# A new order for the 2,617 steps of a fused attention and two-layer feed-forward kernel

## The chip, the cores and the metric

The kernel runs on one core of one Trainium2 chip, as one program. The metric is the time of the whole program on the device, in microseconds (us).

The engines of the core are called by these names: TensorE (PE in the rows, PEld for its weight loads) does the matmuls and the transposes, VectorE (DVE), ScalarE (ACT) and GpSimd (POOL) the elementwise work, and SyncE (SP) issues the DMAs. Each engine takes its own instructions strictly in the order of the program and waits on semaphores for the others.

## The reference, cut to what matters

```python
# q, k, v: 4 batches, 8 heads, 576 positions, 64 values; m = 32 landmarks
q_lm, k_lm = (x.reshape(B, H, m, S // m, D).mean(axis=3) for x in (q, k))
A  = softmax(scale * q    @ k_lm.T)      # 576 x 32
Bm = softmax(scale * q_lm @ k_lm.T)      # 32 x 32
C  = softmax(scale * q_lm @ k.T)         # 32 x 576
Z  = Bm.T / (norm1(Bm) * norminf(Bm) + 1e-06)
for _ in range(6):
    Z = 2 * Z - Z @ Bm @ Z
attn = A @ Z @ C @ v                     # -> x: 2304 tokens x 512

h = x @ w_in                             # first layer, 512 -> 2048
y = (h * tanh(log1p(exp(h)))) @ w_out    # 2048 -> 512
h = y @ w_in2                            # second layer
out = square(maximum(h, 0)) @ w_out2
```

## The kernel before, in words

The whole kernel is one list of short steps, the string PROGRAM at the top of the file. The last loop of the kernel takes the steps from left to right and calls the method that each names: `t11.e1` is method `e(1)` of object `t11`. A step issues from one to some tens of instructions, mostly on one engine. So the order of the list is the order of the instructions on every engine, TensorE's, VectorE's, ScalarE's and GpSimd's queues and SyncE's DMA queue alike; nothing else orders the work. What follows an `@` names the kind of PSUM buffer that a TensorE step takes, and `+n` puts n matmuls without use ahead of it.

Buffers are handed out while the list is run: a step that needs one takes the one that has been free for longest (`take`, line 253), and the step that reads last gives it back (`give`). There are 25 pages of 128x768 numbers (39 later), 24 buffers for weights, and five of PSUM: two of kind h, two of kind y, one of kind at. A step that takes a buffer waits on the chip until the readers of its former contents are done.

The objects are these.

- **a to h**: the eight groups of four heads. Loads (lk, lq, lv), sums for the landmarks (sk, sq), transposes on TensorE (tk, tq, tl, pe), scores and products (pa, pb, pc, pv), softmax and scaling on VectorE, ScalarE and GpSimd (cm, ce, at, am, mi, ae, su, mu, tb, ah, al).
- **B0, B1, B2**: the small inverse for batch 0, for batch 1, and for batches 2 and 3. nr, rs and bs prepare it; n0 to n5 are the Newton steps on TensorE, each with an r on ScalarE (line 747) and a z on VectorE (line 751); pw and wz finish it.
- **F00 to F33**: folds of the attention into the first layer's weights, for a batch and a quarter of the hidden units: fo on TensorE (line 797), mh on ScalarE, ml on VectorE (line 808).
- **U0 to U63**: weights of both layers. d loads one (SyncE); lo and ab (ScalarE, lines 329 and 338), st (VectorE, line 332) and cl (VectorE, lines 342 and 343) mend its bits, ad adds the halves on GpSimd; hi and lw split it into a high and a low part.
- **t0 to t23**: the first layer, by quarter of the hidden units and by tile of 384 tokens. f0 to f3 are matmuls into an h buffer, M the activation, c and g (line 885) the split in two parts, y0 to y3 the second matmuls, each into a y buffer, and e0 to e3 (line 926 on VectorE for most) add a y buffer to the sum and free it. With two y buffers, y3 waits for e1, and y0 of the next turn for e2.
- **W, K, X**: sums and differences of the second layer's weights (W0 to W7, K0 to K7) and of its input (X0 to X2). Their l steps are long subtractions on GpSimd (lines 953 and 992), the t steps of X differences on VectorE (line 983).
- **Q, Y, Z**: the second layer in three passes over the tokens. Qpj loads weights (a, b), does seven products P on TensorE (p1 to p7, lines 1191 to 1193) and adds them on VectorE (d1 to d7). Ypm loads weights (b), prepares its input (r, t on line 1064, h on ScalarE, l on GpSimd on line 1087), does seven products O (p1 to p7) and adds them (a1 to a7). Zp ends a pass and stores. Each O product is 18 matmuls and each P product 6.
- **x**: e and m load ScalarE's tables for Exp and Mish ahead of their use; two frees the buffers of the first half.

Every product is made of three matmuls of high and low parts (`prod`, lines 811 to 814).

Of the kernel before, what the change touches and what calls it, by code (L numbers as in the profile page):

```python
# [10 lines left out]
F32 = mybir.dt.float32  # L11
F32R = mybir.dt.float32r
U32 = mybir.dt.uint32
# [41 lines left out]
    B0.n2@at+2 U3.ab U2.cl f.lk B0.r2 c.Sk c.tl@y B0.z2 U3.cl c.TL d.tk@h a.tb U3.ad a.cv U7.ab b.pv@y+1 d.sk d.lv
    b.ae U2.ad a.ah c.pb@at B0.n3@y+2 c.PB d.Tk c.pc@h U7.cl c.lv B0.r3 d.Sk B0.z3 b.cr U7.ad B0.n4@y c.cm b.cv
    e.tk@h B0.r4 a.al B0.z4 c.ce b.su B0.n5@y d.tl@y d.TL c.pa@at e.lv B0.z5 U7.hi B0.pw@y+3 e.Tk c.at U7.lw d.pb@y
    c.am U5.lo d.pc@at b.mu U4.hi B0.wz d.cm F00.fo@h U4.lw b.tb d.ce e.sq b.ah d.pe@at b.al U8.d F00.mh f.tk@h+4
    f.lv d.PB d.ET d.pa@at F00.ml B1.bx B1.be d.pv@y U6.lo U5.st t0.f0 B1.bs U6.st c.mi B1.nr@y f.Tk e.Sq c.ae B1.rs
# [5 lines left out]
    h.lv U9.lo U11.st d.mu f.at d.tb F10.mh f.pc@h e.pa@at f.cm f.pb@y c.al d.ah U11.ab F10.ml t0.y3 f.ce U11.cl
    e.at e.pe@h t0.e3 f.PB d.al t1.f0 U9.st e.ET t1.f1 t1.f2 U9.ab g.lk t1.M0 e.cr t1.f3 f.pe@h t1.c0 t1.M1 U9.cl
    f.ET g.lq g.tk@at U11.ad t1.c1 U10.d f.am e.am U9.ad f.cr t1.g0 U10.lo t1.g1 U13.d U10.st g.Tk t2.f0 t2.f1
    U13.lo U10.ab e.mi e.pv@y U13.st e.cv f.pv@y g.tq@at U13.ab U10.cl U10.ad e.ae t1.y0 U13.cl f.cv U12.d t2.f2
    g.sk f.mi t2.f3 t1.e0 U13.ad t1.y1 g.sq t2.M0 F01.fo@h U13.hi g.Tq e.su g.Sk U12.lo g.Sq t1.e1 F01.mh U13.lw
# [20 lines left out]
    K1.v3 U23.ab t9.f1 K1.h1 t7.y0 t7.y1 K1.l0 t8.M1 U23.cl U40.lo U23.ad U40.st t7.e0 t7.e1 U23.hi K1.sv0 t9.f2  # L90
    U40.ab t7.y2 U23.lw t7.y3 U41.d U40.cl t7.e2 t8.c1 t7.e3 t8.g0 t8.g1 F31.ml U40.ad U22.d t9.f3 U41.lo t9.M0
    U41.st t8.y0 U41.ab U41.cl K1.l1 t8.y1 t9.M1 U41.ad t10.f0 K1.sv1 t8.e0 U22.lo U22.st U24.d U22.ab W2.v0 t8.e1
    t9.c0 t8.y2 U22.cl t8.y3 U22.ad t9.c1 t9.g0 U22.hi t8.e2 U24.lo t8.e3 t10.f1 t10.f2 U22.lw W2.v1 U24.st t10.f3
    W2.v2 U24.ab t9.g1 t10.M0 U31.d U31.lo U24.cl U31.st t11.f0 t9.y0 W2.v3 t10.M1 t11.f1 U24.ad U31.ab U31.cl x.m
    W2.h1 U26.d U31.ad t9.e0 t9.y1 U31.hi U26.lo t9.e1 t10.c0 W2.l1 t9.y2 U31.lw t9.e2 t10.c1 W2.sv1 U26.st t10.g0
    t11.f2 U16.d U26.ab t9.y3 U26.cl t11.f3 W2.h0 U26.ad t10.g1 W2.l0 t11.M0 t9.e3 U44.d t10.y0 W2.sv0 U16.lo U16.st
    t11.c0 U16.ab t10.e0 U16.cl U16.ad U45.d t10.y1 t10.y2 F02.fo@at t10.e1 t11.M1 U44.lo U44.st U44.ab t10.e2
    U44.cl t10.y3 F02.mh U45.lo F02.ml t11.g0 U44.ad t12.f0 U45.st t11.c1 U27.d t12.f1 U45.ab F12.fo@at F12.mh
    t11.g1 t10.e3 K2.v0 t11.y0 U45.cl F12.ml U27.lo U45.ad U27.st U27.ab K2.v2 t12.f2 t11.y1 t11.e0 t12.M0 U27.cl
# [5 lines left out]
    U46.st t12.y3 W3.l0 t12.e2 U46.ab W3.sv0 t14.M0 U47.lo U46.cl t13.y0 F32.mh t15.f0 t14.c0 U46.ad U47.st t12.e3
    U47.ab U28.d t14.M1 t15.f1 W3.h1 t13.e0 W3.l1 U47.cl U28.lo Q00.a0 t13.y1 t15.f2 t13.y2 t14.g0 t14.c1 F32.ml
    t13.e1 U47.ad U28.st K3.v0 t13.e2 F03.fo@at W3.sv1 t13.y3 K3.v1 U28.ab U28.cl Q03.a0 U28.ad U28.hi U28.lw K3.v3
    t15.M0 t15.f3 t13.e3 t14.g1 t14.y0 t14.e0 t15.c0 K3.v2 t15.M1 U48.d U48.lo t14.y1 U48.st K3.h1 t16.f0 t16.f1
    U49.d t14.e1 U48.ab t15.c1 U49.lo U48.cl U49.st K3.l1 t15.g0 t15.g1 t14.y2 K3.sv1 U48.ad t14.y3 U29.d U49.ab
# [1215 lines left out]
```

## Time and profile before

| | before |
|---|---|
| median of 3 runs | 796.95 us (791.98 to 797.18) |
| the profiled execution | 794.81 us |
| its span, first to last instruction | 793.0 us |
| TensorE busy | 763.4 us, 96% |
| VectorE busy | 613.5 us, 77% |
| ScalarE busy | 408.0 us, 51% |
| GpSimd busy | 439.0 us, 55% |
| mean granted TensorE clock | 0.997 |

The profiled execution is one run of the program. Its span leaves out 1.8 us around the first and the last instruction. TensorE's busy time is that of overlapping matmuls whose ends are modelled, so a busy TensorE is not always one at its full rate; a row of the profile gives the idle time of an engine just before an instruction and what ended it.

### The profile page before, as it was taken

The page shows a single profiled execution, that of the slowest core. Times are in us where ns is not written, and L with a number is a line of the kernel's source. Part 1 is how long each engine was busy: PE and PEld are TensorE (multiplying, and loading weights), DVE is VectorE, ACT ScalarE, POOL GpSimd, SP SyncE. Part 2 cuts the span into 40 slices and gives each one's busy share as a digit, 9 for nine tenths or more (in the row PEclk, how much of TensorE's full clock was granted, in tenths as well). Part 3 has the DMA queues.
Part 4 walks back from the last instruction along what each step waited for, and adds up shares of the span by engine and source line. Part 5 has one row for each costly group of instructions (what it writes and reads, how often), then busy time and mean ns, then how long its engine had stood idle before and what let it go on. Part 6 is the DMA issues. An engine that isn't in the chain of part 4 may idle for free.

```text
span 793.0 us, 15868 instructions
## 1 busy us (share of the span) xinstructions
PE 763.4 (96%) x6094; PEld 720.3 (91%) x6094; DVE 613.5 (77%) x920; ACT 408.0 (51%) x630; POOL 439.0 (55%) x287
## 2 busy tenths in 40 slices
...
GB/s 288 294 196 68 166 136 106 122 147 217 164 178 173 170 214 173 228 178 264 277 297 200 350 258 253 213 263 262 225 276 326 247 239 242 231 269 309 272 78 80
DMA packets 95596, 171.45 MB, mean 216 GB/s; under 512 B 10016, under 2 KB 37664, under 8 KB 95520
## 3 DMA queue, kind: packets, MB, share of 16 engines
...
q10 hardware_dynamic: 576, 0.79, 0.4%
...
q14 instruction: 28, 0.23, 0.1%
...
## 4 chain that ended last, share of the span: by engine, by line
PE 68%; DMA 10%; DVE 8%; ACT 7%; POOL 3%; issue 3%; SPq 0%; DVEq 0%; ACTq 0%; POOLq 0%
PE O L813 8%; PE O L814 8%; PE O L812 8%; PE P L1191 7%; PE P L1192 7%; PE P L1193 7%; DMA rawwi<-in_moe_w_in_dram 6%; PE y L812 5%; PE y L813 4%; PE y L814 4%; DMA rawwo<-in_moe_w_out_dram 3%; PE h L812 2%; PE h L814 2%; PE h L813 2%; DVE rawwi L332 1%
## 5 line engine op out<-in xcount | busy, mean ns | idle before, releaser
L1087 POOL TENSOR_TENSOR glr<-A,ghr 128x768 fp32r<-128x768 f32 x77 | 157.4, 2067 | 125.4 <-ACT ghr L1082 105.0
L812 PE MATMUL O<-b,ghr 128*128 128x256 f32 x462 | 130.3, 282 | 0.7 <-ACT ghr L1082 0.7
L813 PE MATMUL O<-b,ghr 128*128 128x256 f32 x462 | 130.5, 282 | 0.0
L814 PE MATMUL O<-b,glr 128*128 128x256 f32 x462 | 130.5, 282 | 0.0
L1082 ACT CAST ghr<-A 128x768 fp32r<-128x768 f32 x77 | 62.3, 835 | 117.8 <-DVE A L1064 48.8
L812 PEld LDWEIGHTS O<-b,ghr 128*128 128x128 f32 x462 | 87.9, 190 | 1.0 <-ACT ghr L1082 1.0
L813 PEld LDWEIGHTS O<-b,ghr 128*128 128x128 f32 x462 | 88.0, 190 | 0.3 <-DMA b<-sc 0.3
L814 PEld LDWEIGHTS O<-b,glr 128*128 128x128 f32 x462 | 88.2, 191 | 0.0
L812 PE MATMUL h<-ah,mh 128*128 128x384 f32 (+1 forms) x256 | 79.0, 309 | 0.0
L814 PE MATMUL h<-ah,ml 128*128 128x384 f32 (+1 forms) x256 | 78.0, 305 | 0.0
L813 PE MATMUL h<-al,mh 128*128 128x384 f32 (+1 forms) x256 | 78.0, 305 | 0.0
L1221 DVE TENSOR_TENSOR A<-U,P 128x384 f32<-128x384 f32 x88 | 47.9, 549 | 30.8 <-PE P L1193 29.2
L1221 DVE TENSOR_TENSOR U<-U,P 128x384 f32<-128x384 f32 x72 | 39.6, 551 | 39.7 <-PE P L1193 39.1
L885 DVE TENSOR_TENSOR gl<-s,gh 128x768 fp32r<-128x768 f32 x48 | 55.7, 1164 | 6.5 <-ACT gh L875 6.5
L1059 DVE SCALAR_TENSOR_TENSOR A<-A 128x768 f32<-128x768 f32 x44 | 52.4, 1202 | 0.1
L1113 DVE SCALAR_TENSOR_TENSOR sum<-O,sum 128x768 f32<-128x768 f32 x50 | 47.2, 951 | 6.5 <-PE O L814 6.5
L812 PEld LDWEIGHTS h<-ah,mh 128*128 128x128 f32 x256 | 48.5, 190 | 4.0 <-issue 2.5
L926 DVE TENSOR_TENSOR acc<-acc,y 128x384 f32<-128x384 f32 x72 | 38.9, 547 | 16.7 <-PE y L814 16.7
L953 POOL TENSOR_TENSOR ws<-ws,wh 128x1024 fp32r<-128x1024 f32 x16 | 41.2, 2573 | 18.0 <-ACT wh L949 17.9
L1064 DVE TENSOR_TENSOR A<-A,A 128x768 f32<-128x768 f32 x44 | 49.8, 1131 | 1.2 <-PE P L1193 0.9
L814 PEld LDWEIGHTS h<-ah,ml 128*128 128x128 f32 x256 | 48.6, 190 | 0.1
L813 PEld LDWEIGHTS h<-al,mh 128*128 128x128 f32 x256 | 48.6, 190 | 0.0
...
## 6 DMA issues: line engine op xcount, KB each, us to landing
b<-sc SPq DMA_DIRECT2D x154, 256.0 KB, 4.0
...
rawwi<-in_moe_w_in_dram SPq DMA_DIRECT2D x48, 256.0 KB, 4.1
...
```

The source lines that it names most:

```text
L812: nc.tensor.matmul(ps, wh, rh, start=start, stop=False)
L813: nc.tensor.matmul(ps, wh, rl, start=False, stop=False)
L814: nc.tensor.matmul(ps, wl, rh, start=False, stop=stop)
L885: nc.vector.tensor_tensor(self.gl[:, sl, :], self.s[hf], self.gh[:, sl, :].bitcast(F32), ALU.subtract)
L1059: nc.vector.scalar_tensor_tensor(c, c, 0.0, c, ALU.max, ALU.mult)
L1064: nc.vector.tensor_tensor(self.room(to), self.A[x], self.A[y], op)
L1082: nc.scalar.copy(self.form(k)[0], self.A[self.src(k)])
L1087: nc.gpsimd.tensor_tensor(lo, self.A[self.src(k)], hi.bitcast(F32), ALU.subtract)
L1191: nc.tensor.matmul(ps[:, :TT], wh[:, c], xh[:, c, :], start=c == 0, stop=False)
L1192: nc.tensor.matmul(ps[:, :TT], wh[:, c], xl[:, c, :], start=False, stop=False)
L1193: nc.tensor.matmul(ps[:, :TT], wl[:, c], xh[:, c, :], start=False, stop=c == 1)
L1221: nc.vector.tensor_tensor(to, x, self.ps[i][:, :TT], ALU.add)
```

## The change

Only the string PROGRAM changes. It holds the same 2,617 steps, each with the same kind of PSUM buffer and the same `+n`, so the same instructions; the methods, the pools and the number of buffers are the same. The first 53 steps and the last 14 stay where they are. The order of the others was made from durations in the trace of the kernel before. Since buffers are handed out in the order of the list, which buffer a step gets can differ.

Of TensorE's 553 steps 311 have another place among them, one place away on average; of VectorE's 747 steps 521 (two places), of ScalarE's 573 steps 442 (two), of GpSimd's 268 steps 127 (less than one), and of SyncE's 468 steps with DMAs 393 (eight places on average, 63 at most).

All lines of the string but the first two differ. These are the lines of the diff that hold the steps of which the prediction speaks, first of the old order, then of the new one:

```diff
--- before.py
+++ after.py
@@ -48,165 +48,165 @@
...
-    b.ce d.lk B0.nr@y b.at d.tq@h B0.rs c.tq@at+2 d.Tq b.lv a.su c.Tq b.am U3.lo e.lk B0.n0@at+5 U7.st b.mi c.sq
...
-    B1.z4 B1.n5@at e.TL e.pc@h c.su B1.z5 t0.g1 U8.cl e.pb@at U8.ad B1.pw@y t0.y0 f.Sq U11.d B1.wz f.sk t0.y1 e.PB
...
-    t3.e2 B2.nr@y t5.M0 h.pe@h B2.rs t3.y3 B2.n0@at W0.l0 U36.cl B2.r0 g.su U36.ad B2.z0 B2.n1@y U37.d t5.c0 W0.sv0
...
-    U42.cl t13.f1 t11.e1 U20.st t12.g0 U20.ab U42.ad t12.c1 U20.cl K2.h1 t11.e2 U30.d t11.y3 t11.e3 U20.ad t13.M0
-    U20.hi t12.g1 Q01.a2 t13.f2 t13.c0 t13.f3 F22.fo@at t14.f0 t14.f1 U20.lw U43.d U30.lo U30.st t13.M1 t13.c1
-    U30.ab t12.y0 t14.f2 U30.cl F22.mh t13.g0 U43.lo K2.l1 U30.ad U30.hi U43.st F22.ml U43.ab t12.y1 F32.fo@at
...
-    U29.ab U29.cl K3.l0 F03.mh t16.g0 U52.lo U29.ad W4.v3 U29.hi W4.v2 K3.sv0 U29.lw t16.M1 t15.e0 U52.st t15.y1
-    t17.f1 t15.e1 F03.ml W4.h0 W4.l0 U53.d t15.y2 W4.h1 t16.c1 x.e t17.M0 t15.y3 t17.f2 t17.f3 t16.g1 U52.ab t15.e2
...
-    t18.f2 K4.v0 K4.v1 K4.v2 U51.lo t17.g1 t16.y3 K4.v3 K4.l0 K4.sv0 U51.st t17.y0 U50.ab U50.cl Q00.a3 t18.M0
-    U50.ad U51.ab t16.e3 U51.cl U51.ad t17.e0 F23.fo@at U54.d t18.f3 W5.v0 t18.c0 t17.y1 U55.d W5.v1 W5.h0 W5.v2
...
-    t18.e2 U57.ab K5.sv1 U57.cl U56.ab K5.l0 t18.e3 K5.sv0 t19.y0 U56.cl U56.ad U57.ad t19.e0 t19.y1 Q00.a1 t19.y2
...
-    t23.f0 Q00.a5 t20.e2 U63.st X0.h2 U62.ab t21.y0 U62.cl U63.ab t20.e3 U63.cl t21.y1 U62.ad K7.v0 U63.ad t22.M1
-    U58.d t21.e0 t22.c0 t22.g0 t21.y2 K7.v1 t21.e2 t22.c1 t21.e1 X0.t3 K7.h0 t22.g1 X0.h6 t23.f1 t23.M0 K7.v2 U58.lo
...
-    U59.st t22.y2 t23.g0 K7.sv0 x.e X0.t2 t22.e1 U58.cl K7.l1 t22.e2 t23.M1 t23.c1 Y00.b12 U58.ad t22.y3 t23.g1
...
-    Y03.h5 Y02.a3 x.e Q11.p5 Y03.l5 Y03.l1 Y02.a7 Q11.d4 Q11.p3 Q12.a6 X2.h0 Y03.p1@h Y02.a6 Q13.a4 Q11.d5 Q11.d7
...
-    Y10.t1 Y11.b12 Q15.a3 Q13.p7 Q13.d2 Y10.h3 Y10.l3 Y10.t3 Q13.d3 Q13.p4 Q13.d6 Q13.p5 Q13.d4 Y10.a4 Q13.d5 Y10.h5
...
-    Q20.a1 Y12.l3 Y12.b8 Y12.b3 Y12.b11 Y12.p1@h Q17.p6 Y11.a6 Y11.p3@h Q17.d2 Q17.a1 Y12.t2 Y12.h4 Q17.p5 Y12.a1
-    Y12.b5 Y12.p5@h Q17.d3 Y13.b0 Q17.p4 Q17.d4 Y12.l1 Q17.d5 Y12.t4 Q20.p1 Y13.b7 Y11.a3 Q17.d6 Q21.a5 Y12.p2@at
...
+    U4.ad c.Tk B0.nr@y c.tq@at+2 c.Tq a.su d.tq@h B0.rs b.am U4.hi b.ce d.lk U7.st U5.d b.lv e.lk U6.d@gh B0.n0@at+5
...
+    e.TL B1.z4 B1.n5@at c.su B1.z5 e.pc@h t0.g1 U11.d e.pb@at U8.cl B1.pw@y t0.y0 e.PB B1.wz d.ae U8.ad f.sk c.mu
...
+    h.ET U36.cl B2.rs t5.M0 t3.y3 t3.e3 W0.l0 W0.sv0 U21.st B2.n0@at B2.r0 h.pv@y B2.z0 g.su B2.n1@y B2.r1 B2.z1
...
+    U27.ab U27.cl t11.y1 F12.mh U27.ad F12.ml U20.d t12.c0 t11.y2 F22.fo@at U42.lo K2.v2 U42.st t13.f0 t11.e1 t13.f1
+    U42.ab t11.y3 t12.M1 t11.e2 t12.c1 U42.cl U20.lo U20.st U20.ab t12.g0 U20.cl K2.l0 U42.ad t13.M0 U20.ad t13.c0
...
+    F22.mh t13.M1 U43.lo F22.ml U30.ad U43.st U30.hi U43.ab K2.l1 t14.f1 t12.y0 K2.sv1 t12.y1 t13.c1 U30.lw t12.e1
+    t14.f2 t12.e0 U46.d U43.cl U43.ad W3.v0 t13.g1 t14.f3 F32.fo@at t12.y2 W3.h0 t14.M0 t14.M1 t12.y3 W3.v2 U46.lo
...
+    W4.v0 t14.e3 Q00.a3 t15.y0 U29.ab t15.y1 K3.sv0 W4.v1 t16.M1 t16.c1 U52.d t17.f2 U29.cl F03.ml U29.ad W4.v2
+    t15.e1 U29.hi U52.lo t15.y2 U29.lw U53.d W4.v3 W4.h1 W4.h0 W4.l1 t15.e0 t16.g1 W4.l0 t17.f3 U52.st t15.e2 t15.y3
...
+    t16.y3 K4.v2 U51.d U50.lo t17.y0 t18.f2 t18.f3 K4.v3 U50.st F13.ml K4.l0 U50.ab U50.cl U51.lo U50.ad U51.st
+    t17.e0 t16.e3 U51.ab t18.M0 U51.cl t18.M1 K4.sv0 U51.ad W5.v0 W5.v1 W5.v2 t17.y1 t17.y2 t19.f0 F23.fo@at U54.d
...
+    t19.g1 t20.f2 K5.h0 K5.l1 U57.st t20.M0 K5.sv1 t18.y3 t18.e3 X0.h1 t19.y0 U57.ab t19.y1 K5.l0 t20.f3 U57.cl
...
+    Q01.a6 K6.l0 U62.d K6.sv0 t20.e2 t22.M0 t20.y3 K6.h1 U63.lo K6.l1 K6.sv1 t22.f2 t22.f3 t23.f0 U62.lo t21.y0
+    t20.e3 t23.f1 t22.M1 X0.t2 U62.st U62.ab t22.c0 U63.st U62.cl U62.ad U63.ab t22.g0 t22.c1 K7.v0 t21.e0 t21.y1
+    t21.y2 U63.cl U58.d t21.e1 X0.t1 X0.t3 t21.e2 U63.ad t23.M0 X0.h5 t22.g1 K7.v1 t23.f2 t21.y3 K7.h0 K7.v3 U59.d
...
+    U58.ab U58.cl X0.h4 t23.g0 t22.e1 Q01.a0 t22.y2 t22.e2 t23.g1 t22.y3 Q00.a4 t22.e3 K7.sv0 Q00.a2 K7.h1 X0.l2
+    U59.st t23.y0 t23.e0 t23.y1 K7.l1 U59.ab X0.l6 U59.cl K7.sv1 t23.y2 U58.ad t23.e1 t23.e2 t23.y3 U59.ad X0.l0
...
+    Y10.l2 Q12.d5 Z0.u7 Q13.p6 Z0.f5 Y10.h1 Z0.f4 Y10.p4@h Z0.u4 Q13.a4 Q14.a4 Q13.d2 Z0.o4 Q12.d7 Y11.b2 Q13.p7
...
+    Y12.l0 Y11.b5 Y12.p1@h Y12.t2 Q20.a6 Q17.p7 Q17.d3 Q17.d4 Y12.a1 X2.h6 X2.l6 Q20.a1 X2.l5 Y12.p5@h X2.l4 Q22.a2
...
```

## Rows read from the trace of the kernel before

**Rows 1.** Windows by stage: start:end, us, busy us (instructions) by engine, clock, DMA share

```profile
0.00:17.00 17.00, 10.94 (x78) 8.33 (x79) 11.88 (x12) 8.56 (x16) 2.73 (x12) 1.00 0.91 273
17.00:80.00 63.00, 53.69 (x851) 41.26 (x856) 58.29 (x131) 45.43 (x100) 25.55 (x24) 0.97 0.72 196
80.00:430.00 350.00, 340.89 (x2711) 317.03 (x2696) 270.51 (x400) 238.65 (x356) 207.88 (x153) 1.00 0.58 186
430.00:760.00 330.00, 329.15 (x2296) 328.13 (x2295) 250.59 (x347) 112.79 (x157) 194.26 (x96) 1.00 0.81 265
760.00:793.00 33.00, 28.75 (x173) 25.57 (x171) 22.28 (x33) 2.52 (x3) 8.56 (x4) 0.98 0.19 50
```

**Rows 2.** Waits of TensorE, 430 to 793 us: who and for whom, total us, times, longest

```profile
PE O L812 <- ACT ghr L1082: 0.7, 1, 0.7
```

**Rows 3.** Waits of TensorE, 80 to 430 us, the five largest

```profile
PE y L812 <- DVE acc L926: 3.4, 4, 1.2
PE nw__2124 L734 <- DVE inv L751: 1.0, 1, 1.0
PE nw__2300 L734 <- ACT inv L747: 0.9, 1, 0.9
PE m L797 <- DVE ml L808: 0.7, 1, 0.7
PE nw__2151 L734 <- DVE inv L751: 0.7, 1, 0.7
```

**Rows 4.** Timeline, four short windows, VectorE and GpSimd: start us, us, engine, line, instruction

```profile
264.66 2.23 DVE L342 TENSOR_SCALAR rawwi<-rawwi 128x512 f32<-128x512 f32 x1 [0.77 <-ACT rawwi L338]
...
264.20 2.40 POOL L953 TENSOR_TENSOR wa<-wa,wh 128x1024 fp32r<-128x1024 f32 x1 [0.87 <-ACT wh L949]
...
366.37 2.89 DVE L332 SCALAR_TENSOR_TENSOR rawwi<-rawwi 128x512 uint32<-128x512 uint32 x1
...
366.19 2.52 POOL L953 TENSOR_TENSOR ws<-ws,wh 128x1024 fp32r<-128x1024 f32 x1 [1.17 <-ACT wh L949]
...
415.45 1.65 DVE L332 SCALAR_TENSOR_TENSOR rawwi<-rawwi 128x512 uint32<-128x512 uint32 x1 [0.67 <-ACT rawwi L329]
...
414.14 2.41 POOL L953 TENSOR_TENSOR ws<-ws,wh 128x1024 fp32r<-128x1024 f32 x1 [3.98 <-ACT wh L949]
...
636.97 2.31 DVE L1064 TENSOR_TENSOR A<-A,A 128x768 f32<-128x768 f32 x1
...
636.61 1.85 POOL L992 TENSOR_TENSOR fl<-acc,fh 128x768 fp32r<-128x768 f32 x1
```

**Rows 5.** Waits of TensorE, 17 to 80 us, the largest

```profile
PE nrm L701 <- DVE inv L693: 1.8, 1, 1.8
```

**Rows 6.** Timeline of TensorE: the first matmuls of a y, an f and a y step

```profile
276.02 0.33 PE L812 MATMUL y<-gh,wo_8h 128*128 128x384 f32 x1
...
278.10 0.33 PE L812 MATMUL h<-ah,mh 128*128 128x384 f32 x1
...
279.14 0.33 PE L812 MATMUL y<-gh,wo_8h 128*128 128x384 f32 x1
```

**Rows 7.** Single lines of the kernel on VectorE: count, ns minimum/median/maximum, starts, forms

```profile
L332 DVE SCALAR_TENSOR_TENSOR rawwi<-rawwi x32: 629/696/2890, 11.3 to 415.5; 128x512 uint32<-128x512 uint32 x32
...
L342 DVE TENSOR_SCALAR rawwi<-rawwi x32: 409/428/2228, 17.4 to 424.3; 128x512 f32<-128x512 f32 x32
...
L343 DVE TENSOR_SCALAR rawwi<-rawwi x32: 427/430/435, 17.9 to 425.9; 128x512 uint32<-128x512 uint32 x32
...
L885 DVE TENSOR_TENSOR gl<-s,gh x48: 943/953/2532, 64.7 to 420.5; 128x768 fp32r<-128x768 f32 x48
...
L983 DVE TENSOR_TENSOR t<-acc,t x6: 946/952/3089, 397.7 to 625.4; 128x768 f32<-128x768 f32 x6
...
L926 DVE TENSOR_TENSOR acc<-acc,y x72: 516/547/556, 133.3 to 430.1; 128x384 f32<-128x384 f32 x72
```

**Rows 8.** The page's DMA issues: line, queue, count, KB each, us to landing

```profile
b<-sc SPq DMA_DIRECT2D x154, 256.0 KB, 4.0
```

More of the change, by code (lines that the diff above doesn't have):

```diff
@@ L55 @@
[L55 to L59, printed above, removed]
@@ L65 @@
[L65 to L69, printed above, removed]
@@ L90 @@
[L90 to L99, printed above, removed]
@@ L105 @@
[L105 to L109, printed above, removed]
@@ L110 @@
-    U49.cl t16.M0 t16.f2 K3.h0 t16.c0 t14.e3 U29.lo t16.f3 U49.ad t17.f0 t14.e2 U29.st W4.v0 W4.v1 U52.d t15.y0
-    U29.ab U29.cl K3.l0 F03.mh t16.g0 U52.lo U29.ad W4.v3 U29.hi W4.v2 K3.sv0 U29.lw t16.M1 t15.e0 U52.st t15.y1
-    t17.f1 t15.e1 F03.ml W4.h0 W4.l0 U53.d t15.y2 W4.h1 t16.c1 x.e t17.M0 t15.y3 t17.f2 t17.f3 t16.g1 U52.ab t15.e2
-    t15.e3 W4.sv0 U52.cl U53.lo W4.l1 t16.y0 F13.fo@at U53.st U53.ab U53.cl F13.mh t17.c0 t16.y1 t16.e0 t17.g0
-    W4.sv1 t16.y2 t17.M1 U52.ad U50.d U53.ad U50.lo F13.ml t18.f0 K4.h0 t16.e2 U50.st t17.c1 t18.f1 t16.e1 U51.d
@@ L120 @@
-    t19.g0 t18.y1 t18.y2 t19.c1 t18.e1 K5.h1 t20.f1 t20.M0 Q00.a4 K5.h0 U56.st t18.y3 t20.f2 t19.g1 K5.l1 U57.st
-    t18.e2 U57.ab K5.sv1 U57.cl U56.ab K5.l0 t18.e3 K5.sv0 t19.y0 U56.cl U56.ad U57.ad t19.e0 t19.y1 Q00.a1 t19.y2
-    W6.v0 W6.v1 W6.v3 t20.c0 Q05.a2 U60.d W6.h0 W6.v2 X0.h0 t19.e2 W6.l0 t20.f3 U61.d W6.h1 W6.l1 F33.fo@at t19.y3
-    t20.M1 W6.sv1 W6.sv0 t20.g0 t19.e3 t20.c1 t19.e1 t21.f0 U60.lo t21.f1 U61.lo t20.g1 Q01.a0 U60.st X0.h1 U61.st
-    U60.ab U61.ab U60.cl U60.ad K6.v0 t21.M0 t20.y0 U61.cl F33.mh U62.d U61.ad t21.c0 K6.v1 U63.d F33.ml K6.v2
@@ L125 @@
-    t20.y1 Q01.a1 t21.f2 t20.e1 t21.g0 x.e x.m K6.v3 K6.h0 t21.f3 K6.l0 t21.M1 K6.sv0 t22.f0 t22.f1 t20.e0 K6.h1
-    K6.l1 Q03.a5 t21.c1 X0.t0 t22.M0 K6.sv1 t22.f2 U62.lo U62.st X0.t1 t20.y2 t22.f3 t20.y3 t21.g1 Q01.a4 U63.lo
-    t23.f0 Q00.a5 t20.e2 U63.st X0.h2 U62.ab t21.y0 U62.cl U63.ab t20.e3 U63.cl t21.y1 U62.ad K7.v0 U63.ad t22.M1
-    U58.d t21.e0 t22.c0 t22.g0 t21.y2 K7.v1 t21.e2 t22.c1 t21.e1 X0.t3 K7.h0 t22.g1 X0.h6 t23.f1 t23.M0 K7.v2 U58.lo
-    t21.y3 X0.l6 t23.f2 t23.f3 K7.v3 U59.d t21.e3 K7.h1 K7.l0 U58.st t23.c0 t22.y0 t22.y1 U59.lo U58.ab t22.e0
@@ new lines @@
+    t13.y2 t15.f2 t13.e1 t15.M0 t13.e2 t13.y3 t15.f3 W3.sv1 U28.st U28.ab t14.g1 t16.f0 K3.v1 K3.v3 U28.cl Q01.a2
+    t15.c0 t13.e3 U28.ad F03.fo@at U28.hi t14.y0 K3.v2 U48.d t14.y1 K3.h1 U28.lw t15.M1 t14.e0 U48.lo t14.y2 U48.st
+    t15.g0 t16.f1 t15.c1 U48.ab U48.cl t16.f2 U49.d t15.g1 t14.e1 t16.f3 K3.l1 K3.h0 K3.sv1 Q01.a1 U49.lo t16.M0
+    U48.ad U49.st t14.y3 F03.mh U49.ab t14.e2 t17.f0 t16.c0 U49.cl U29.d U29.lo K3.l0 t16.g0 U29.st U49.ad t17.f1
+    W4.v0 t14.e3 Q00.a3 t15.y0 U29.ab t15.y1 K3.sv0 W4.v1 t16.M1 t16.c1 U52.d t17.f2 U29.cl F03.ml U29.ad W4.v2
@@ new lines @@
+    t15.e1 U29.hi U52.lo t15.y2 U29.lw U53.d W4.v3 W4.h1 W4.h0 W4.l1 t15.e0 t16.g1 W4.l0 t17.f3 U52.st t15.e2 t15.y3
+    t17.M0 t15.e3 U53.lo U52.ab x.m t17.M1 t17.c0 t16.y0 U53.st U53.ab t18.f0 U52.cl t16.e0 F13.fo@at U53.cl W4.sv1
+    t16.y1 U52.ad t17.g0 t16.y2 F13.mh t17.c1 U53.ad K4.v0 t18.f1 W4.sv0 K4.h0 K4.v1 t16.e1 t17.g1 t16.e2 U50.d
+    t16.y3 K4.v2 U51.d U50.lo t17.y0 t18.f2 t18.f3 K4.v3 U50.st F13.ml K4.l0 U50.ab U50.cl U51.lo U50.ad U51.st
+    t17.e0 t16.e3 U51.ab t18.M0 U51.cl t18.M1 K4.sv0 U51.ad W5.v0 W5.v1 W5.v2 t17.y1 t17.y2 t19.f0 F23.fo@at U54.d
@@ new lines @@
+    t17.e1 U55.d t18.c0 W5.v3 W5.h0 W5.l0 W5.sv0 t17.y3 t19.f1 Q02.a3 U54.lo U54.st t18.c1 U55.lo t18.g0 U54.ab
+    t19.f2 W5.h1 U54.cl U55.st W5.l1 U55.ab Q01.a4 t19.M0 t17.e2 U54.ad t18.g1 t19.c0 W5.sv1 K4.h1 U55.cl t19.f3
+    t18.y0 t17.e3 t19.g0 U55.ad K4.l1 U56.d F23.mh F23.ml t19.M1 K5.v0 t20.f0 K5.v1 U56.lo t19.c1 U57.d t18.e0
+    U56.st U56.ab t18.y1 t18.y2 t18.e2 K5.v2 K4.sv1 F33.fo@at K5.v3 t18.e1 K5.h1 U57.lo x.e U56.cl Q03.a0 t20.f1
+    t19.g1 t20.f2 K5.h0 K5.l1 U57.st t20.M0 K5.sv1 t18.y3 t18.e3 X0.h1 t19.y0 U57.ab t19.y1 K5.l0 t20.f3 U57.cl
```

236 lines of the change are left out of this document (130 added, 106 removed).

## The prediction

> **What bounds the kernel now.** I read the table of windows first [rows 1]. The reader is to see that TensorE is the engine that sets the end, and how little of its time is idle: 6.06 us up to 17 us, 9.31 us from 17 to 80, 9.11 us from 80 to 430, 0.85 us from 430 to 760 and 4.25 us at the end, 29.6 us in all. The first 53 steps and the last 14 keep their places. The 53 run to about the end of the first stretch, so that stretch stays as it is, and so does most of the last one, which holds the stores after the last matmul. What an order can win at all is the idle time of the three stretches between, 9.31 + 9.11 + 0.85 = 19.3 us, 2.4% of the span.
>
> The lists of what TensorE waited for come next. From 430 us on there is one wait of 0.7 us [rows 2]: half of the program runs at TensorE's own rate, and no order makes that shorter. From 80 to 430 us the list adds up to 9.0 us; its five largest lines are four waits of a y step for a VectorE add that frees the y buffer (3.4 us), three of the Newton steps of B2 (1.0, 0.9 and 0.7 us), and a fold that waits for the ml of the fold before it (0.7 us) [rows 3].
>
> Then the timeline of VectorE and GpSimd just ahead of these waits [rows 4]. Steps are put to instructions by counting the instructions of their line in the program's order. U42.cl has its first instruction at 264.66 and takes 2.23 us; K2.l0 on GpSimd runs from 264.20 to 266.60. U57.st takes 2.89 us beside K5.l1 (366.19 to 368.71), U59.st 1.65 us beside K7.l1 (414.14 to 416.55), Y12.t2 2.31 us beside an X2.l step (to 638.46). Each time the VectorE step ends within 0.9 us of GpSimd's end, and behind it in VectorE's queue stands the step that TensorE waits for: t11.e1, t18.e2 and t18.e3, t22.e1, Y12.a1.
>
> **From 17 to 80 us.** VectorE is busy for 58.29 of these 63 us [rows 1], more than TensorE with 53.69, so it sets the pace. In the two lists the VectorE steps ahead of B0.bs are the same 17, those ahead of B1.wz the same 72, those ahead of F10.ml the same 81: what has to be done before the Newton steps and the first folds is the same sum of durations. The largest wait here, 1.8 us of nrm for B0.bs [rows 5], therefore stays. The order can only win VectorE's own idle time, 63 - 58.29 = 4.7 us, or lose as much if the chains of the Newton steps fall worse. In the new order n2 and n3 of B0 stand back to back, where before it was n0 and n1; n2 and n3 of B1, back to back before, get e.tq between them. I take 0, between -4.7 and +4.7. This also covers the loads U6.d and d.lk, which change places in SyncE's queue here, since nothing at the top of VectorE's or TensorE's waits in this stretch is a DMA.
>
> **From 80 to 430 us, what goes.** TensorE's steps have fixed lengths while nothing is late: a y step takes 278.10 - 276.02 = 2.08 us and an f step on one batch 279.14 - 278.10 = 1.04 us [rows 6]. Before, t11.e1 is queued behind U42.cl; after, ahead of it. t22.e1 was behind U59.st, and is now ahead. t18.e2 was behind U57.st and is ahead; t18.e3 is still behind it. So three of the four y waits have lost their cause: 3/4 of 3.4 us is 2.6 us. F22.ml stood 3 steps ahead of F32.fo and now stands 21 ahead, with t12.y0 and t12.y1 between, so the 0.7 us of the fold goes. For B2 the order was n0, n1, n2, pe, n3; it is n0, pv, n1, pe, n2, n3. The two back-to-back pairs that waited 1.0 and 0.7 us become one, so about 0.8 us goes. Together 4.1 us.
>
> **What comes.** Three places are packed more tightly than before. At t21.y2 the buffer is freed by t21.e0, and between t21.y0 and t21.e0 VectorE now has t20.e3, X0.t2, U62.st, U63.st, U62.cl, t22.g0 and t21.e0. By the medians [rows 7] that is 0.55 + 0.95 + 0.70 + 0.70 + 0.86 + 0.95 + 0.55 = 5.26 us, and TensorE covers it with t21.y0, one f step and t21.y1, 2.08 + 1.04 + 2.08 = 5.20 us. Before, U62.cl, t20.e3, U63.cl and e0 stood there, 2.82 us, against 4.16. The other two are t17.y1 (U50.st, F13.ml, U50.cl, U51.st ahead of t17.e0) and t15.y2 (U29.cl and F03.ml ahead of t15.e1, with one f step to cover). The nearest row is t22.y3 before: VectorE had 0.55 + 0.70 + 0.95 + 0.95 + 0.55 = 3.70 us against 4.16, one step stood 1 us longer, and TensorE waited about 1 us of the 3.4 [rows 3]. So each of the three costs between nothing, if VectorE is ahead at that point, and 2.2 us, if a step there takes the longest time of its line instead of the median (2.89 - 0.70) [rows 7]. I take 0.7 us for each, 2.1 us in all.
>
> The durations differ because of what runs beside, and an order made from them carries them to other places: line 332 took from 0.63 to 2.89 us, line 342 from 0.41 to 2.23 us, for one shape [rows 7]. The add of line 926, which reads PSUM, took 0.52 to 0.56 us each of 72 times. [...]
>
> **From 430 us on.** TensorE does 2296 matmuls in 329.15 us, 0.143 us each [rows 1]. The one wait lies behind Y12.t2; after, Y12.t2 comes right behind Y12.p1, without Q17.p6 and Y11.p3 between, and X2.l6 and X2.l5 come behind it. I take -0.5 of the 0.7 us. SyncE's queue is what changes most here (393 of its 468 steps move, by eight places on average, against one place for TensorE and two for VectorE). A 256 KB load lands 4.0 us after its issue [rows 8]. The shortest lead that I find by counting TensorE's steps between the last reader of a buffer and the use of the load is that of Q13.a4: Y03.p2 frees its buffer, and 6 + 6 + 18 = 30 matmuls, 4.3 us, lie before Q13.p7. That costs 0 to 0.5 us; I take 0.3. All other leads are above 6 us. GpSimd (127 of 268 steps moved, by less than one place on average) is busy for 194.26 of 330 us and keeps its order of use. ScalarE changes between Exp and Mish as often in the new list as in the old one, so no table load is added.
>
> **The sum.** 0 - 4.1 + 2.1 - 0.5 + 0.3 = -2.2 us against the profiled execution's 794.81 us (span 793.0 and 1.8 around it), so 792.6 us. That execution lies 2.1 us below the median of the three runs, 796.95; set against the median the sum gives 794.7 us, and I say 794.5.
>
> **The rivals.** First, the new order takes nearly every wait away: the 9.1 us of the middle stretch, the 0.85 us, and half of VectorE's 4.7 us of idle time, -12 us, 785 us. For it speaks that four of the large waits are undone at their place; against it, that the tightest places are now packed to 0.1 us and that the two lists of VectorE agree at so many points up to B1.wz. Second, the order changes nothing that counts: each of the sets ahead of t3.g1, t6.g1 and t8.g1 on VectorE is the same before and after, waits move to neighbours, and the time is within 2 us of 797. Third, slower: VectorE is late at the steps that free TensorE's buffers. Place: t15.e1, t17.e0 and t21.e0, and the like places around the folds. Price: 3 x 2.2 = 6.6 us there, with the 4.1 us coming back in front of other e steps because the same long steps still meet GpSimd's, and 2 us more between 17 and 80 us: about +8 us, 805 us. It decides as soon as VectorE comes to such a place with less than a y step, 2.08 us, in hand.
>
> **How the numbers follow.** My forecast, -2 us with the second rival as its neighbour, holds 0.62 together with it; the first rival has 0.23, the third 0.15. No change and a change can hardly be told apart below 1%, about 8 us here. Those are the chances of the same, faster and slower. The range reaches to the first rival's 785 us and near to the third's 805: 784.5 to 804, which also takes in the +-4.7 us of the stretch up to 80 us.
>
> **What would show it.** The waits of y for the add of line 926 should fall from 3.4 us to about 1 plus what t15, t17 and t21 add; the fold's wait should be gone; B2 should have two Newton waits left; from 430 us on TensorE should stay at 0.143 us per matmul. I would be wrong if the stretch from 17 to 80 us changes by over 5 us, if a load shows among TensorE's waits, or if the waits of 80 to 430 us pass 12 us.

## The result, and the profile after

The new order took 801.96 us (median of 6 runs, 800.45 to 803.31), the order before 795.45 us (6 runs, 791.98 to 797.18): a ratio of 1.0088, with a 95% interval from 1.0060 to 1.0117. It lies within 1%, inside the range of the prediction, and on the wrong side: 6.5 us longer, where 2.5 us shorter was forecast. The profiled execution took 800.45 us, with a span of 798.7.

The table of windows by stage of the kernel after answers to [rows 1], with the same columns:

```profile
0.00:17.00 17.00, 9.98 (x85) 7.71 (x85) 12.41 (x13) 8.77 (x17) 2.72 (x12) 0.90 0.92 277
17.00:80.00 63.00, 53.57 (x894) 41.42 (x895) 59.37 (x135) 47.21 (x103) 29.09 (x27) 1.00 0.69 197
80.00:430.00 350.00, 344.09 (x2682) 321.76 (x2682) 270.21 (x403) 237.20 (x353) 205.22 (x150) 1.00 0.60 191
430.00:760.00 330.00, 322.80 (x2238) 320.68 (x2237) 245.96 (x336) 110.49 (x154) 191.72 (x94) 0.99 0.80 257
760.00:798.70 38.70, 33.23 (x201) 29.50 (x199) 26.91 (x37) 4.81 (x6) 9.71 (x5) 1.00 0.24 66
```

The reader is to see two numbers. From 80 to 430 us TensorE's idle time fell from 9.11 to 350 - 344.09 = 5.91 us, more than the forecast's 2.0 us net. From 430 to 760 us, where it was 0.85 us and no order seemed able to do anything, it is 330 - 322.80 = 7.20 us.

What TensorE waited for from 430 us to the end (engine, line, who ended the wait: total us, times, longest) is three lines, where [rows 2] had one:

```profile
PE P L1191 <- ACT U L1201: 7.1, 1, 7.1
PE O L812 <- PE O L814: 0.7, 1, 0.7
PE O L812 <- DVE sum L1113: 0.4, 1, 0.4
```

One single wait of 7.1 us is new and large; the experiments below show that it, with the slow matmuls behind it, is the loss. The list for 80 to 430 us answers to [rows 3]; of its eleven lines these are the ones that the prediction speaks of, and the first is new:

```profile
PE nw__2194 L734 <- issue: 1.9, 1, 1.9
PE nw__2194 L734 <- DVE inv L751: 0.8, 1, 0.8
PE nw__2096 L734 <- DVE inv L724: 0.7, 1, 0.7
...
PE h L814 <- DVE ml L808: 0.4, 1, 0.4
...
PE y L812 <- DVE acc L926: 0.2, 1, 0.2
PE m L797 <- DVE ml L808: 0.2, 1, 0.2
```

The timeline around the long wait, one engine after the other (start us, us, engine, line, instruction; in brackets the idle time before it and what ended it; SPq is SyncE's queue of transfers):

```profile
436.32 0.34 PE L1193 MATMUL P<-fh,q01w 128*128 128x384 f32 x1
443.79 0.69 PE L1191 MATMUL P<-fh,q00w 128*128 128x384 f32 x1 [7.12 <-ACT U L1201]
444.27 0.52 PE L1192 MATMUL P<-fl,q00w 128*128 128x384 f32 x1
444.59 0.52 PE L1193 MATMUL P<-fh,q00w 128*128 128x384 f32 x1
...
434.85 0.83 ACT L1082 CAST ghr<-A 128x768 fp32r<-128x768 f32 x1 [3.27 <-DVE A L1059]
443.25 0.48 ACT L1201 COPY U<-P 128x384 f32<-128x384 f32 x1 [7.57 <-DMA st<-ws]
...
435.76 2.06 POOL L1087 TENSOR_TENSOR glr<-A,ghr 128x768 fp32r<-128x768 f32 x1 [3.26 <-ACT ghr L1082]
437.78 2.34 POOL L953 TENSOR_TENSOR ws<-ws,wh 128x1024 fp32r<-128x1024 f32 x1
...
435.62 0.38 SPq L965 DMA_DIRECT2D st<-wh  x1
440.14 0.32 SPq L966 DMA_DIRECT2D st<-ws  x1
```

Read it backwards. TensorE stands from 436.66 to 443.79 because ScalarE's copy at 443.25 has to free its PSUM buffer (step Q00.p5 takes the buffer that Q03.s frees). ScalarE had nothing to do since 435.68; its copy waited for a transfer, "st<-ws", which is the store of the buffer ws7, the last store of the first half (step W7.sv1). That store was issued at 440.14, behind GpSimd's 2.34 us on the same buffer (W7.l1), which stood in GpSimd's queue behind the 2.06 us of Y00.l0. By the view of its line it landed 2.9 us after its issue, at about 443.0, and the copy ran 0.2 us later.

Why should a copy of U03, a page of the second half, wait for the store of ws7? The step x.two hands the memory of the first half to 14 new pages, and they are laid in it in the order of their first use (e1 and e2 below change that order and nothing else). A page has 2 x 384 numbers of 4 bytes, 3,072 bytes in each partition; U03 is the third page, bytes 6,144 to 9,216. In the memory of the first half two m buffers of 512 x 2 x 4 = 4,096 bytes come first, and the buffer T0 begins at byte 8,192. So U03 lies over the beginning of T0. Before, T0 held wh70, stored early, and ws7 was in T2; after, ws7 is in T0. No step chose that: T buffers are handed out in turn, and the steps that take them and give them back stand in another sequence in the new list (W6.sv0, for one, ahead of W6.sv1 instead of behind it).

In the kernel before, the same copy had no such wait, though the last store was issued only 0.57 us earlier on the clock (ScalarE's and SyncE's timeline of before):

```profile
440.52 0.48 ACT L1201 COPY U<-P 128x384 f32<-128x384 f32 x1 [3.51 <-PE P L1193]
...
439.57 0.32 SPq L966 DMA_DIRECT2D st<-ws  x1
```

It ran 0.95 us after the issue, while the store was still on its way (it landed 3.8 us after its issue). A second cost follows the stop: the matmuls from 444.27 to 447.79 start 0.32 us apart, where 0.17 is usual; the 12 that start from 443.79 on fill the 4.00 us to 447.79, where they would take 12 x 0.174 = 2.1, so 1.9 us more. The mean granted clock is 1.00 from 430.0 to 437.0 us, 0.80 from 437.0 to 443.7, 0.53 from 443.7 to 448.0 and 1.00 again from 448.0 to 460.0.

### The profile page after: what moved, and what is told of

The parts are those of the page before. It is cut to its first block, busy times and chain, and to the rows that moved or that the text cites. A ratio compares the mean times of both kernels' runs of the same rounds, so it can differ in the third digit from the quotient of the medians.

```text
span 798.7 us, 15855 instructions
## 1 busy us (share of the span) xinstructions
PE 763.7 (96%) x6094; PEld 721.1 (90%) x6094; DVE 614.9 (77%) x920; ACT 408.5 (51%) x630; POOL 438.5 (55%) x287
## 4 chain that ended last, share of the span: by engine, by line
PE 71%; DVE 13%; DMA 5%; issue 4%; ACT 4%; POOL 2%; SPq 0%; DVEq 0%; ACTq 0%; POOLq 0%
PE O L812 8%; PE O L814 8%; PE O L813 8%; PE P L1191 7%; PE P L1193 7%; PE P L1192 7%; PE y L812 6%; PE y L813 5%; PE y L814 5%; PE h L812 2%; PE h L814 2%; PE h L813 2%; DMA rawwo<-in_moe_w_out_dram 2%; DMA rawwi<-in_moe_w_in_dram 2%; PE m L797 1%
## 5 line engine op out<-in xcount | busy, mean ns | idle before, releaser
L1064 DVE TENSOR_TENSOR A<-A,A 128x768 f32<-128x768 f32 x44 | 56.9, 1294 | 0.1
L1059 DVE SCALAR_TENSOR_TENSOR A<-A 128x768 f32<-128x768 f32 x44 | 47.9, 1100 | 0.1
```

Of the source, the lines that this page charges most:

```text
L1059: nc.vector.scalar_tensor_tensor(c, c, 0.0, c, ALU.max, ALU.mult)
L1064: nc.vector.tensor_tensor(self.room(to), self.A[x], self.A[y], op)
```

## The experiments

Theory 1 says that the loss is this hand-over of memory. Rival 2 says that W7's last steps and x.two stand too late in the new list, wherever the page lies. Rival 3 says that the new order costs over its whole length. The runs e1 to e11 were timed in five rounds, in three groups (e1 to e4, e5 to e8, e9 to e11), each beside the kernel before, whose median was 794.02, 794.52 and 794.42 us; the change itself is the run of the result, beside 795.45 us. So the ratios compare, and the times only to about 1 us. The last column is from the one profiled execution of each run.

```
run                                  us    ratio to before, 95% interval   stop at U03 or U02
after (the change)                   801.96  1.0088  1.0060 to 1.0117       7.12
e1 after, other places for pages     792.29  0.9981  0.9966 to 0.9996       none
e2 before, U03 put over ws7          797.34  1.0030  1.0015 to 1.0046       2.40
e3 after, Y00.l0 later               800.76  1.0083  1.0061 to 1.0106       4.82
e4 after, W7's last steps earlier    795.04  1.0007  0.9990 to 1.0024       1.44
e5 after, K6.sv0 8 places later      794.09  0.9984  0.9969 to 0.9999       1.61
e6 after, W6.sv0 6 places later      800.40  1.0062  1.0038 to 1.0086       4.56
e7 before to step 1240, then after   794.79  0.9998  0.9983 to 1.0013       none
e8 after to step 1240, then before   797.55  1.0032  1.0018 to 1.0045       1.36
e9 e1 with t5.f2 ahead of B2.n3      788.86  0.9942  0.9920 to 0.9964       none
e10 e1 with h.pv behind t5.f3        788.58  0.9929  0.9918 to 0.9941       none
e11 before, B2's row as after        795.97  1.0023  1.0009 to 1.0036       none
```

**Only the places of the pages (e1, e2).** No instruction moves; the pages are laid out ahead of their use. The edit of e1, to the new order (e2 puts another order of numbers into the same lines, in the kernel before):

```
             free["pg"].extend(range(25, 25 + MORE))
+            for i in (25, 26, 37, 38, 27, 28, 29, 30, 31, 32, 33, 34, 35, 36):
+                l2.tile([P, 2, TT], F32, tag=f"pg{i}", name=f"at{i}")
```

> The new order, every instruction as it is; only the 14 pages of the second half get other places in the memory of the first: the third page (U03, written by Q03.s) lies over ml33, whose readers were done long before, and no longer over ws7, whose store is the last one of the first half. Theory 1 (Q03.s waits because its page lies over ws7, the buffer that the last store W7.sv1 still reads): TensorE's stop of 7.1 us at 436.7 us is gone, and so are the 13 matmuls at half clock behind it (0.32 us apart where they were 0.17: 1.8 us): 802.0 - 8.9 = 793, between 791.5 and 794.5. Rival 2 (W7.l1, W7.sv1 and x.two come too late in the order, wherever the page lies): 802, the stop stays at 7.1. Rival 3 (the new order costs over its whole length, the stop only replaces other idle time): above 798.

> The order before, every instruction as it is; only the pages are laid so that U03 (Q03.s) comes to lie over ws7, which it didn't. Theory 1: the copy of Q03.s, at 440.5 us in the profile of before, must wait until the last store, issued at 439.6, has landed some 3 us later: TensorE stops for about 2 us where it had no wait: 797.5, between 796.5 and 799. Rival 2: no change, 795.5. Rival 3: no change, 795.5.

Both came out as theory 1 has it: 792.29 us, and 797.34 us. In e1 the waits from 430 us on are the two small ones of after, and the copy of Q03.s runs at 438.33 although the store of ws7 is issued 4.6 us behind it (waits, then ScalarE's and SyncE's timeline of e1):

```profile
PE O L812 <- PE O L814: 0.7, 1, 0.7
PE O L812 <- DVE sum L1113: 0.4, 1, 0.4
...
438.33 0.47 ACT L1201 COPY U<-P 128x384 f32<-128x384 f32 x1
...
442.97 0.32 SPq L966 DMA_DIRECT2D st<-ws  x1
```

In e2 a wait appears in a kernel that had none (waits of TensorE from 430 us on). The row of its copy names no transfer, but the store of ws7, issued at 438.81, landed 3.7 us later and the copy ran at 442.61, 0.1 us behind it:

```profile
PE P L1191 <- ACT U L1201: 2.4, 1, 2.4
```

So the order of the last steps alone (rival 2) costs nothing where the page lies elsewhere, and the place of the page alone makes the stop in the old order. Rival 3 falls too: with the pages moved, the new order is no slower than the old one; it is 0.2% faster, with an interval that ends just below 1.

**The store earlier, the page left where it is (e3, e4).** e3 moves one step, e4 three:

```
 e3:  ... W7.h1 Y00.h0 Q02.a1 [-Y00.l0-] W7.l1 W7.sv1 {+Y00.l0+} x.two ...
 e4:  ... W7.v3 {+W7.h1+} ... W7.l0 {+W7.l1+} ... W7.sv0 {+W7.sv1+} ...
      ... Y00.r0 [-W7.h1-] Y00.h0 Q02.a1 Y00.l0 [-W7.l1 W7.sv1-] x.two ...
```

> The new order with one step moved: Y00.l0 on GpSimd comes behind W7.l1 and W7.sv1, not ahead of them; U03 still lies over ws7. GpSimd stood idle from 432.5 to 435.8 us, waiting for the input of Y00.l0. Theory 1: W7.l1 starts at 432.5, its store is issued at 436.0 behind the one before it and lands at 439: the stop shrinks from 7.1 to about 2.9 us, not to nothing; 797, between 795.5 and 798. Rival 2: the stop is gone, 793. Rival 3: above 798.

> The new order with W7.h1 moved behind W7.v3, W7.l1 behind W7.l0 and W7.sv1 behind W7.sv0; U03 still lies over ws7. Theory 1: the last store is issued at about 435 us and lands at 438, the copy of Q03.s can run at 438 instead of 443.3: a stop of about 1.9 us is left; 796, between 794 and 797.5. Rival 2: the stop is gone, 793. Rival 3: above 798.

e4 did what theory 1 said: a stop of 1.44 us, 795.04 us. e3 missed its number: 800.76 us lies where rival 3 put it. Its trace tells why (the waits; then, by the view of the tile ws, the issue of the last store and its time to landing):

```profile
PE P L1191 <- ACT U L1201: 4.8, 1, 4.8
...
L966 SPq DMA_DIRECT2D st<-ws x1: 371/371/371, 438.7 to 438.7; - x1
...
DMA to landing us min/median/max: 5.7/5.7/5.7
```

This execution came to the place 2.8 us later than that of after (the copy at 425.93 us there is at 428.75 here), though the two lists are the same up to there; the granted clock was 0.95 here and 1.00 there from 17 to 80 us, and 0.90 and 0.95 from 140 to 175 us.

With that shift, the issue at 438.7 is the 436.0 that I had put, and what failed is the landing: 5.7 us after the issue instead of 2.9. The store follows right behind four loads, issued from 436.26 on, and the other half of W7.sv1. The stop shrank only to 4.82 us, 1.9 more than I had put, and the matmuls behind it were slow as after the 7.12, another 2.1 us that I had left out: 797 and these two make 801.0, so rival 3 is not needed for it. The row of this copy names the load of q05w as what ended its wait; by its own view that load landed at 445.0, behind the copy at 444.64, and the store at 444.4. That neither e3 nor e4 made the stop go also speaks against rival 2.

**One far step moved (e5, e6).** K6.sv0 and W6.sv0 give T buffers back long before the stop:

```
 e5:  U62.d [-K6.sv0-] t20.e2 t22.M0 t20.y3 K6.h1 U63.lo K6.l1 K6.sv1 t22.f2 {+K6.sv0+} t22.f3
 e6:  t21.f2 [-W6.sv0-] W6.l1 X0.h0 U60.ab t21.c0 U60.cl W6.sv1 {+W6.sv0+} t20.y0
```

> The new order with one step of 2617 moved 8 places back, some 80 us ahead of the stop: K6.sv0, which gives two T buffers back. Every later T buffer is handed out in another turn: now wa7 lies under U03 (its store is issued at 432.9 us in the profile of after, and lands 2.4 later, before Q03.s needs the page), and ws7 under U02, which the trace of the run with other places writes 5.6 us after U03. Theory 1: the stop of 7.1 us at Q03.s is gone; at U02 some 2 us can stand instead: 794, between 792 and 796. Rival 2 (W7 too late in the order, wherever the buffers lie): 802, as the steps around the stop are untouched. Rival 3: above 798.

> The new order with another single step moved: W6.sv0 6 places back, behind W6.sv1, as it stood before. ws7 moves out from under U03, but wh71 comes under it; its store is issued at 435.6 us in the profile of after, 4.5 us ahead of that of ws7, and landed 5.4 us later there (3.8 in the profile of before). Theory 1: Q03.s waits until 439.4 to 441.0, a stop of 3.3 to 4.9 us with the clock falling at the upper end: 798, between 795 and 799.5. Rival 2: 802. Rival 3: above 800.

e5 came out at 794.09 us; the stop at U03 is gone, and the predicted one stands at U02, now the page over ws7 (TensorE's and ScalarE's timeline of e5):

```profile
445.84 0.45 PE L1191 MATMUL P<-fh,q02w 128*128 128x384 f32 x1 [1.61 <-ACT U L1201]
...
445.31 0.48 ACT L1201 COPY U<-P 128x384 f32<-128x384 f32 x1 [7.25 <-DMA st<-ws]
```

e6 took 800.40 us, 0.9 us above its range: the store of wh71, now under U03, landed 5.2 us after its issue at 437.93, and the stop was 4.56 us, near the upper end, with slow matmuls behind it (e1's 0.9981, with 4.56 us of stop and 2.5 of slow matmuls added, makes 1.0070, within the interval around the 1.0062 that was measured). The profile of e5 also has 2.4 us more of y waits than after (lines 926 and 922), which theory 1 does not explain; their cause is open. Moving one step of 2,617 by eight places changed the time by about 8 us, more than all the forecast's terms together; rival 2 has no room for that.

**Half of one order, half of the other (e7, e8).**

```
 e7:  PROGRAM = the first 1240 steps of the order before + all other steps in the new order
 e8:  PROGRAM = the first 1240 steps of the new order + all other steps in the order before
```

> The first 1240 steps in the order before, the other 1377 in the new order, so the steps around the stop and all of the second half stand as in the new order; only the turn of the T buffers comes from the order before: wa7 and wh70 lie under U03 and U02, both stored early. Theory 1: no stop; the waits of the middle stretch are back, as most of it is in the order before: 795, between 793 and 797. Rival 2 (the steps around x.two stand badly in the new order): 802. Rival 3: between 795 and 802, by how much of the loss lies in the second half.

> The first 1240 steps in the new order, the rest in the order before. wh71 comes under U03; its store is issued at 438.3 us in the profile of before and lands 3.8 later, the copy of Q03.s stood at 440.5 there. Theory 1: the shorter waits of the middle stretch, and a stop of about 1.7 us at Q03.s: 794.5, between 793 and 796.5. Rival 2: no stop, 792.5. Rival 3 (the loss lies in the first part of the new order): above 798.

e7 has every step around x.two as in the new order, and no stop: 794.79 us. e8 has the predicted stop (1.36 us), but 797.55 us is 1 us above its range: the y steps waited 3.0 us for the add of line 926, 2.4 of them in one wait just behind the seam, at 375 us.

**What is left in the middle stretch (e9 to e11).** The seven kernels so far with the new first part (after, e1, e3 to e6, e8) show the line "nw__2194 <- issue", 1.8 to 2.1 us inside B2.n3. TensorE's timeline of e1 there:

```profile
151.10 0.41 PE L734 MATMUL nw__2194<-inv 32*32 32x64 f32 x11 [0.76 <-DVE inv L751]
153.58 0.85 PE L734 MATMUL nw__2194<-inv 32*32 32x64 f32 x21 [2.07 <-issue]
154.36 0.69 PE L812 MATMUL h<-ah,mh 128*128 128x384 f32 x1
154.85 0.52 PE L813 MATMUL h<-al,mh 128*128 128x384 f32 x1
155.17 0.52 PE L814 MATMUL h<-ah,ml 128*128 128x384 f32 x1
```

Eleven of the 32 short matmuls run, then 2.07 us pass in which TensorE waits for no engine and no transfer that the profile shows, and the long matmuls behind it start 0.32 us apart. The order before had n0, n1, n2, g.pe, n3 with two waits for VectorE between, 1.0 and 0.7 us [rows 3], and nothing like this stop. The edits:

```
 e9  (on e1):      B2.n2@y B2.r2 U36.ad B2.z2 {+t5.f2+} B2.n3@y [-t5.f2-] U37.d
 e10 (on e1):      B2.n0@at B2.r0 [-h.pv@y-] B2.z0 g.su B2.n1@y ... t5.f3 {+h.pv@y+} U37.lo
 e11 (on before):  t3.y3 {+t3.e3+} B2.n0@at ... B2.z0 {+h.ET h.pv@y+} B2.n1@y ... B2.z1 {+g.pe@at+} B2.n2@y [-h.ET g.pe@at t3.e3-] ...
```

> The run with other places for the pages (new order, no stop at Q03.s), with one more step moved: t5.f2, 6 long matmuls, comes between B2.n2 and B2.n3, not behind n3. In every run of the new order TensorE stops for 0.8 us ahead of B2.n3 (waiting for VectorE) and again for 1.8 to 2.1 us behind the 11th of its 32 matmuls, waiting for nothing that the profile shows, and the matmuls behind it run 0.32 us apart instead of 0.17. Theory A (161 short matmuls stand in a row there, B2.n0, h.pv, B2.n1, g.pe, B2.n2, B2.n3, and TensorE is not supplied fast enough): the long matmuls break the row, both stops go, and the clock stays up: 2.1 + 0.8 + 3.5 for some 24 slow matmuls, 6 us less than the run with other places: 787, between 785 and 790. Theory B (the place in the program decides, whatever stands around it): the second stop stays at about 2 us a few instructions further, 791.5.

> The run with other places for the pages, with h.pv (48 short matmuls) moved from between B2.n0 and B2.n1 to behind t5.f3, so that n0, n1, g.pe, n2 and n3 stand in a row as they nearly did before. Theory A: 113 short matmuls up to the place of the stop, as in the order before, which had no stop there; the stop of 2 us and the half clock go, the waits for VectorE ahead of n1 and n2 (1.0 and 0.7 us before) come back: 788.5, between 786.5 and 791. Theory B: the stop stays, 792 to 794.

> The order before, with only the short matmuls of B2 put in the new row: h.ET and h.pv between B2.n0 and B2.n1, g.pe between n1 and n2, n2 and n3 back to back (t3.e3 comes earlier, as h.pv needs its buffer). Theory A: a stop of about 2 us inside B2.n3 and half clock behind it, 3 us more than before after the waits of 1.0 and 0.7 us that this order fills: 797.5, between 795.5 and 800. Theory B: no such stop, 794.

e9 gained 0.4% on e1 and e10 0.5%, both near theory A's times; they are the fastest kernels of this study and beat both orders. But e9's trace doesn't bear theory A out as I put it (TensorE's timeline of e9):

```profile
148.86 0.30 PE L734 MATMUL nw__2201<-inv 32*32 32x64 f32 x5
150.45 0.63 PE L734 MATMUL nw__2201<-inv 32*32 32x64 f32 x27 [1.29 <-issue]
151.01 0.44 PE L812 MATMUL h<-ah,mh 128*128 128x384 f32 x1
151.29 0.34 PE L813 MATMUL h<-al,mh 128*128 128x384 f32 x1
```

The stop is still there, 1.29 us, and now behind the 5th matmul of n3. With the 6 of t5.f2 ahead, that is the same 11 matmuls behind n2: the place in the instruction stream is theory B's, only the length is shorter. By the windows TensorE has begun 1,747 matmuls and 1,748 weight loads of the program when it stops, in after, e1 and e9 alike. The list of transfers shows one block for an instruction queue ahead of each stop, by 0.3 to 1.2 us (queue, kind: packets, MB, share; first e1 from 151.00 to 151.25 us, then e9 from 148.00 to 148.25):

```profile
q8 instruction: 1, 0.02, 23.4%
...
q8 instruction: 1, 0.02, 22.0%
```

TensorE goes on 2.6 and 2.5 us behind the start of that window, and in the kernel after 2.5 us behind it as well (148.50 and 150.95). The whole program has 6,094 matmuls and 6,094 weight loads and 48 blocks of this queue, 0.79 MB in all (16.5 KB each), so 254 of these instructions for a block. The stop of 0.6 us without a releaser that e10 has, in n5, stands behind 1,874 matmuls and 1,875 weight loads: 254 instructions further, one block.

A stop at the end of a block of TensorE's code, ended by the arrival of the next block and as long as TensorE is early for it, fits these counts and times. That is a reading of them: no row of a trace names the block as what ended the stop, and no run here changes the blocks alone.

e11 is a miss: in the old order the same row of short matmuls got no such stop, but waits of 1.08, 0.65 and 0.76 us for other engines, and 795.97 us. That time lies inside theory A's range, but not for its reason. In e11 the block of this place came just ahead of 149.50 us and of n1 (151.50), with 244 matmuls and weight loads begun since the one before it, as many as in the kernel before (130 + 114 in the window from 137.98 to 148.61 us, between two blocks); in after, e1 and e9 it came after 460 to 487 (after: 234 + 226 from 134.75 to 148.63). A row of short matmuls alone doesn't make the stop; why the block came so much later in the new order stays open.

Of what e10 gained the clock is the larger part. The windows of 10 us around this place (columns as in [rows 1]), of e1, and of e10:

```profile
150.00:160.00 10.00, 7.17 (x141) 6.13 (x134) 3.97 (x14) 4.15 (x9) 4.24 (x5) 0.66 0.18 68
```

```profile
150.00:160.00 10.00, 8.87 (x224) 7.48 (x224) 6.75 (x18) 8.05 (x16) 6.80 (x7) 1.00 0.37 104
```

The granted clock is 0.66 in e1 and 1.00 in e10. The 12 long matmuls behind the stop of e1, 0.32 us apart where 0.174 is usual, cost 1.75 us more, and two rows of short ones some 0.7. In e10 the waits for VectorE ahead of n1 and n3 are back (0.7 and 0.8 us), and with the stop of 0.6 us they are 2.1 us, against 0.8 + 2.07 in e1, so 0.7 us less. The two together are about 3.2 us of the 4.1 by which the ratios differ. How e9's 3.1 us divide is not shown as clearly: its stop is 0.8 us shorter, the wait of 0.8 ahead of n3 is gone and its clock stays up (1.00 from 146 to 156 us), but 0.9 and 0.8 us of waits elsewhere are new.

## Why the prediction was wrong

**The step that failed** is "From 430 us on". It counted one wait there, leads of loads, and the queues of the engines, and gave +0.3 and -0.5 us. It asked how early loads are issued, and never which store still reads the memory that a page is laid in: it priced nothing for the hand-over at x.two, though it is known of the kernel that the step frees the buffers of the first half, and of the change that a buffer's turn can differ. The missing term measured 7.12 us of stop and 1.9 us of slow matmuls; e1, which changes only the places of the 14 pages, has a ratio lower by 0.0107, 8.5 us. The row that would have shown it was at hand: the copy of Q03.s in the kernel before ran 0.95 us after the issue of the last store, so it was free only as long as its page lay over something else. None of the three signs of being wrong that the prediction named came up in the profile of after: they looked at the stretch up to 80 us, at loads and at the waits up to 430 us, and not at a store.

**"The sum", -2.2 us,** is what the new order does without that term: e1 is at 0.9981, 1.5 us below the order before, between 0.3 and 2.7. That it comes so near is partly luck, as the terms below were off by up to 1.9 us and cancel.

**"From 80 to 430 us, what goes".** The y waits were put at -2.6 us and fell by 3.2, from 3.4 to 0.2. The fold's wait for ml fell from 0.7 us to 0.2, and an h step now waits 0.4 us for ml. The Newton steps of B2 were put at -0.8 us, as two waits would become one. One was left, as said (0.8 us), and the one of 0.9 went too; but n0 now waits 0.7 us and the stop of 1.9 us is new, so that the sum went up by 0.8, from 2.6 to 3.4, and the slow matmuls behind that stop came on top (granted clock 0.66 from 150 to 155 us). This is the second step that failed: it counted the waits that filling the chain with short matmuls would take away, and priced nothing for a stop without a releaser.

**"What comes", +2.1 us,** measured 0.2: t21.y2, t17.y1 and t15.y2, packed to 0.1 us by the medians, got no wait of 0.7 in the profile of after. Together the two parts were put at -2.0 us; the idle time fell by 3.2, and the slow matmuls behind B2.n3 took part of it back.

**"From 17 to 80 us", 0,** can't be told from the noise. The window of the kernel after holds 894 of TensorE's matmuls, that of the kernel before 851; but e8, with the same list there as after, has 846, at a granted clock of 0.95 where after has 1.00 (the window of e8):

```profile
17.00:80.00 63.00, 54.07 (x846) 42.79 (x854) 57.10 (x130) 45.36 (x99) 28.57 (x26) 0.95 0.71 198
```

At the end of the stop in B2.n3, e1 is 2.6 us behind after (153.58 and 150.95), again with the same list. So executions of one list differ here by as much as the whole sum of the forecast.

**Y12.p5 and Q13.a4.** The wait for ghr [rows 2] is gone as forecast, and two others of 0.7 and 0.4 us stand in its place; no load shows among TensorE's waits in the kernel after. In e6 and e7, with the same list from 430 us on, one wait for a load b<-sc does, 0.5 and 1.0 us, so the 0.3 us were not out of place.

**The rivals.** The third named a time near the one measured, 805 us, and another mechanism, VectorE late at the e steps; the trace shows the contrary (0.2 us at those steps). The right time there is no credit to it. None of the rivals had a step wait for a store.
